# 128 bytes of unused SBUF after kt, in a kernel of band attention and two gated layers

## The chip, the cores and the metric

One core of a Trainium2 chip runs the whole program. The metric is the device time of one execution, in microseconds (us). What is read from the inside of an execution comes from one profiled execution of the kernel.

## What is computed

The reference has three parts. Only the second and third matter for the change, because TensorE (PE) spends most of its time there.

```python
# attention: 2 batches, 8 heads, 768 positions, head size 64: a band of width 16 and 24 block summaries
a = np.exp(scores_all); a = a / (np.sum(a, axis=-1, keepdims=True) + 1e-09)
x = np.matmul(a, v_all)            # then laid out as 1536 tokens x 512
# first gated layer, d_ff 1536
x = ((x @ w_a) * (x @ w_b)) @ w_out
# second gated layer, d_ff 2048
h = x @ w_in
out = (h - np.tanh(h)) @ w_out2
```

All inputs and outputs are float32.

## The kernel before

**Work and stages.** The 1536 tokens are three blocks of 512. A float32 operand of a large product is split into a high and a low part (`fp32r`), and a product of two such operands is three matmuls: high by high, high by low, low by high. One *set* in this document is the 12 matmuls that belong to one piece of 128 hidden columns: 4 slices of 128 by 3 products. Each of the 12 loads 128 x 128 stationary values (LDWEIGHTS, 512 bytes in each partition) and streams 512 moving columns (2,048 bytes in each partition).

- After a head (the first 42 us: loads, attention for the first block) the first layer runs through 3 blocks x 12 pieces. Each piece has three sets: `pos_a` and `pos_b` (both through `proj`, L370: stationary the weight tile `wsp`, moving the activations `XA` or `XB`) and `pos_o` (L398: stationary `wsp`, moving `gh` and `gl`, the high and low part of the gated product). That makes 36 sets at L398. Attention of the later blocks is planned in between.
- The second layer runs through 3 blocks x 16 pieces: `pos_h` (again `proj`, L370) and `pos_o2` (L459: stationary the gated product, moving `wsp`). `pos_h` puts the gated product's two parts into `gh` and `gl` for two pieces of every three, and into two buffers of the tag `vw` for the third (`G % 3 < 2`). That makes 48 sets at L459: 32 with `gh`, `gl` and 16 with `vw`.

```python
for kk in range(KC):
    wh, wl = (s[:, i, kk * 128 : (kk + 1) * 128] for i in range(2))
    for n, (w, xx) in enumerate(((wh, x[:, 0, kk]), (wh, x[:, 1, kk]), (wl, x[:, 0, kk]))):
        mm(dst, w, xx, start=(kk == 0 and n == 0), stop=(kk == KC - 1 and n == 2))
...
gs[1000 + G] = pair((("gh", 2), ("gl", 2)) if G % 3 < 2 else (("vw", 3), ("vw", 3)))
```

**Who makes the operands.** ScalarE (ACT) writes the high part of a weight into `wsp` (L184), VectorE (DVE) or GpSimd (POOL) the low part (L185). ACT writes `gh` (L363), DVE writes `gl` (L364) from `tg` and `gh`. The head is written out by hand (`SEQ`); the rest is ordered by a plan.

**Where the buffers lie.** One pool (`st`) lays a tag's buffers down in the order in which tags are first asked for. `kt` (K transposed, with the block maxima) takes 4 x 792 x 4 = 12,672 bytes in each partition, which is 99 x 128. The built programs place the tiles named in this document at these byte addresses in each partition:

| tag | bytes of a buffer | before | after the change | remainder by 512, before | after |
|---|---|---|---|---|---|
| qn | 2,048 | 18,720 and on | the same | 288 | 288 |
| wsp (4 buffers) | 4,096 | 28,960 and on | the same | 288 | 288 |
| XB | 16,384 | 45,344 | the same | 288 | 288 |
| kw | 2,048 | 61,728 and on | the same | 288 | 288 |
| w | 2,048 | 65,824 and on | the same | 288 | 288 |
| vw (3 buffers) | 2,048 | 139,552 and on | the same | 288 | 288 |
| XA | 16,384 | 145,696 | the same | 288 | 288 |
| kt | 12,672 | 162,080 | the same | 288 | 288 |
| x20a, x20b | 4,096 | 174,752 and on | 174,880 and on | 160 | 288 |
| stage, x21a, x21b | 4,096 | 182,944 and on | 183,072 and on | 160 | 288 |
| e | 2,048 | 203,424 and on | 203,552 and on | 160 | 288 |
| ta, tg | 2,048 | 207,776 and on | 207,904 and on | 416 | 32 |
| gh (2 buffers) | 2,048 | 215,968, 218,016 | 216,096, 218,144 | 416 | 32 |
| gl (2 buffers) | 2,048 | 220,064, 222,112 | 220,192, 222,240 | 416 | 32 |
| at (2 buffers) | 2,048 | 224,160 and on | 224,288 and on | 416 | 32 |

A slice of 128 float32 columns is 512 bytes, so every slice of a tile has its tile's remainder by 512.

Of the kernel before, what the change touches and what calls it, by code (L numbers as in the profile page):

```python
# [39 lines left out]
def band_attention_moe_kernel(ctx: ExitStack, tc: tile.TileContext, q, k, v, w_a, w_b, w_out, w_in, w_out2, out):  # L40
# [22 lines left out]
    def st(shape, tag, bufs=1, dt=F32):  # L63
        return sb.tile(shape, dt, tag=tag, bufs=bufs, name=tag)

    def pt(tag, shape=(128, 512)):
        return ps.tile(list(shape), F32, tag=tag, name=tag)
# [16 lines left out]
    def constants():  # L84
        nc.vector.memset(bsq, -math.sqrt(GA) * GB)
        nc.vector.memset(bth, -GC2)
        nc.vector.memset(qbd2, 0.0)
        nc.gpsimd.memset(qbd3, 0.0)

        for m, n, r in ((mavp, KW + 2 * NB - 8, BLK // 2), (mavg, 2 * NB - 4, BLK)):  # L90
            nc.gpsimd.memset(m, 1.0 / BLK)
            nc.gpsimd.affine_select(
                out=m, in_=m, pattern=[[-r, n]], compare_op=ALU.is_gt, fill=0.0,
                base=(n - NB) * r + 1, channel_multiplier=1,
            )
            nc.gpsimd.affine_select(
                out=m, in_=m, pattern=[[r, n]], compare_op=ALU.is_gt, fill=0.0,
                base=r - (n - NB) * r, channel_multiplier=-1,
            )
        nc.gpsimd.memset(qbd4, 0.0)  # L100
        for m, off in zip(masks, (0, WIN, 2 * WIN)):
            nc.gpsimd.memset(m[:, 0:KW], 0.0)
            nc.gpsimd.memset(m[:, KW:NK], math.log(BLK) / SC)
            for h in range(2):
                band = m[h * 64 : h * 64 + 64, 0:KW]
                nc.gpsimd.affine_select(
                    out=band, in_=band, pattern=[[1, KW]], compare_op=ALU.is_gt, fill=NEG,
                    base=WIN - off, channel_multiplier=-1,
                )
                nc.gpsimd.affine_select(  # L110
                    out=band, in_=band, pattern=[[-1, KW]], compare_op=ALU.is_gt, fill=NEG,
                    base=WIN + off, channel_multiplier=1,
                )
# [659 lines left out]
    with tc.manual_schedule():  # L773
        nc.vector.memset(qbd, 0.0)
        for _ in range(WARM):
            mm(pt("ps")[:, 0:256], qbd[:, 0, 0, :], qbd[:, 0, 0:2, :], start=True, stop=True)
        make_identity(nc, ident)
        XAv = st([128, 4, 2 * TB], "XA")
        kt[0] = st([128, NP, S + NB], "kt")
        constants()  # L780
        for n in SEQ.split():
            exec(compile(f"def op_{n}(op): op('{n}')\n", "<ops>", "exec"), globals())
            globals()["op_" + n](op)
# [50 lines left out]
```

## Time and profile before

| | |
|---|---|
| median of 3 runs | 667.28 us |
| lowest and highest run | 665.36 us, 667.33 us |
| span of the profiled execution (its own time is not listed apart from it) | 664.0 us |
| PE busy | 643.2 us (97%) |
| DVE, ACT, POOL busy | 501.9 us, 476.2 us, 209.7 us |
| PE's share of the chain that ended last | 82% |

The span goes from the first to the last instruction; a run's time is longer by what lies around it. The chain is followed back from the last instruction, at each step to what released it or to the instruction before it on its engine. Matmuls overlap, so the duration of one (some 390 ns) is longer than the time from its start to the next one's; the length of a piece of the chain is the time in which the engine moved on.

### The profile page before, as it was taken

What the parts mean: (1) busy time and instruction counts of PE and PEld (TensorE: products, weight loads), DVE (VectorE), ACT (ScalarE), POOL (GpSimd) and SP (SyncE); (2) the same over time, 40 slices, a digit from 0 to 9 for tenths busy, and PEclk for the clock granted to TensorE, in tenths of its full rate; (3) what the DMA queues carried; (4) which work ended last, traced back from release to release, by engine and by line L of the source; (5) the groups of instructions that cost most, each with busy time, mean ns of one, the idle gap of its engine ahead of it and who ended that gap; (6) DMA issues with size and microseconds to landing.
All of it is one profiled execution on the core that took longest, in us unless ns stands there. A gap on an engine that the chain in (4) does not pass through costs nothing.

```text
span 664.0 us, 9626 instructions
## 1 busy us (share of the span) xinstructions
PE 643.2 (97%) x3240; PEld 518.1 (78%) x3240; DVE 501.9 (76%) x999; ACT 476.2 (72%) x1000; POOL 209.7 (32%) x221
## 2 busy tenths in 40 slices
PE   7778999999899999999999999999999999999997
PEld 5567876888588888888888888888888888888885
DVE  5899999888675777647877748877777877777775
ACT  4899897798677687636655547777777777777774
POOL 6761231122000010101111135554444544444441
PEclk9989999999999999999999999999999999999999
DMA  9996984563414545513444200000010000000001
GB/s 203 243 237 179 250 226 128 169 216 107 102 66 124 169 152 155 144 47 112 149 140 152 68 1 0 1 0 1 1 63 1 0 1 0 32 33 1 1 0 64
DMA packets 84781, 62.11 MB, mean 94 GB/s; under 512 B 51892, under 2 KB 75444, under 8 KB 84732
## 3 DMA queue, kind: packets, MB, share of 16 engines
q1 hardware_dynamic: 84732, 61.50, 33.4%
q8 instruction: 25, 0.41, 0.3%
q14 instruction: 24, 0.20, 0.1%
HBM read 54.00 MB, written 7.34 MB: 92 GB/s over the span
## 4 chain that ended last, share of the span: by engine, by line
PE 82%; DVE 7%; ACT 4%; DMA 3%; issue 2%; SPq 1%; POOL 0%; DVEq 0%; ACTq 0%
PE acc L459 20%; PE pb L370 18%; PE pa L370 17%; PE acc L398 12%; PE pt L370 5%; PE ps L370 5%; DMA stage<-in_moe_w_in_dram 2%; PE ps L288 1%; DVE w L164 1%; PE ps L340 1%; DVE w L165 1%; PE pt L240 1%; PE pt L327 1%; DMA x20a<-in_q_dram 1%; SPq L610 1%
## 5 line engine op out<-in xcount | busy, mean ns | idle before, releaser
L185 POOL TENSOR_TENSOR wsp<-w,wsp 128x512 fp32r<-128x512 f32 x97 | 127.5, 1333 | 143.7 <-ACT wsp L184 143.7
L184 ACT ACTIVATE wsp<-w 128x512 fp32r<-128x512 f32 x201 | 121.4, 622 | 18.8 <-PE acc L398 8.6
L185 DVE TENSOR_TENSOR wsp<-w,wsp 128x512 fp32r<-128x512 f32 x104 | 75.0, 723 | 42.5 <-ACT wsp L184 42.3
L179 POOL TENSOR_SCALAR w<-w 128x512 f32<-128x512 f32 x52 | 42.0, 811 | 184.3 <-ACT w L154 184.1
L398 PE MATMUL acc<-gh,wsp 128*128 128x512 f32 x288 | 97.8, 398 | 0.5 <-ACT gh L363 0.5
L370 PE MATMUL pa<-XA,wsp 128*128 128x512 f32 x336 | 85.0, 400 | 2.8 <-ACT XA L720 2.1
L370 PE MATMUL pb<-XA,wsp 128*128 128x512 f32 x336 | 84.1, 394 | 1.4 <-DVE tg L386 1.4
L459 PE MATMUL acc<-wsp,gh 128*128 128x512 f32 x256 | 80.5, 396 | 0.0
L370 PEld LDWEIGHTS pa<-XA,wsp 128*128 128x128 f32 x336 | 63.5, 191 | 18.3 <-ACT XA L720 2.4
L370 PEld LDWEIGHTS pb<-XA,wsp 128*128 128x128 f32 x336 | 62.1, 188 | 15.0 <-ACT x21a L155 1.6
L363 ACT ACTIVATE gh<-tg 128x512 fp32r<-128x512 f32 x68 | 42.4, 623 | 33.3 <-DVE tg L386 32.9
L398 PEld LDWEIGHTS acc<-gh,wsp 128*128 128x128 f32 x288 | 53.7, 188 | 12.0 <-ACT gh L363 0.6
L370 PE MATMUL pb<-XB,wsp 128*128 128x512 f32 x240 | 61.0, 396 | 0.0
L370 PE MATMUL pa<-XB,wsp 128*128 128x512 f32 x240 | 60.4, 395 | 0.0
L398 PE MATMUL acc<-gl,wsp 128*128 128x512 f32 x144 | 57.3, 399 | 1.1 <-DVE gl L364 1.1
L459 PEld LDWEIGHTS acc<-wsp,gh 128*128 128x128 f32 x256 | 48.2, 188 | 11.1
L364 DVE TENSOR_TENSOR gl<-tg,gh 128x512 fp32r<-128x512 f32 x68 | 46.6, 686 | 9.4 <-ACT gh L363 9.3
L370 PEld LDWEIGHTS pa<-XB,wsp 128*128 128x128 f32 x240 | 44.5, 188 | 9.8 <-DVE XB L348 0.2
L370 PEld LDWEIGHTS pb<-XB,wsp 128*128 128x128 f32 x240 | 44.4, 188 | 9.5
L459 PE MATMUL acc<-wsp,gl 128*128 128x512 f32 x128 | 50.5, 394 | 0.0
L459 PE MATMUL acc<-wsp,vw 128*128 128x512 f32 x192 | 46.5, 390 | 0.0
L459 PEld LDWEIGHTS acc<-wsp,vw 128*128 128x128 f32 x192 | 35.9, 188 | 8.1 <-DVE vw L364 0.4
(304 smaller groups left out, 1176.0 us busy)
## 6 DMA issues: line engine op xcount, KB each, us to landing
stage<-in_moe_w_out_dram SPq DMA_DIRECT2D x19, 512.0 KB, 3.8
stage<-in_moe_w_in_dram SPq DMA_DIRECT2D x16, 512.0 KB, 5.6
stage<-in_moe_w_a_dram SPq DMA_DIRECT2D x8, 512.0 KB, 4.9
w<-wsc SPq DMA_DIRECT2D x16, 256.0 KB, 3.5
vw<-in_v_dram SPq DMA_DIRECT2D x19, 192.0 KB, 3.2
stage<-in_moe_w_b_dram SPq DMA_DIRECT2D x7, 512.0 KB, 5.7
wsc<-x21a SPq DMA_DIRECT2D x8, 256.0 KB, 4.9
wsc<-x21b SPq DMA_DIRECT2D x8, 256.0 KB, 5.1
```

The lines of the kernel that those rows point to most:

```text
L164: nc.vector.scalar_tensor_tensor(r, t[:, :, 1], -0x40000000, r, op0=ALU.bitwise_and, op1=ALU.bitwise_or)
L165: nc.vector.tensor_tensor(r, r, t[:, :, 0], op=ALU.add)
L179: nc.gpsimd.tensor_scalar(rf, rf, HI_HI, HI_LO, op0=ALU.min, op1=ALU.max)
L184: nc.scalar.activation(s[:, 0, :], r, AF.Copy)
L185: eng.tensor_tensor(s[:, 1, :], r, s[:, 0, :].bitcast(F32), op=ALU.subtract)
L240: mm(pp, mavg[:, NB - 4 - 4 * c : 2 * NB - 4 - 4 * c], vch.pop(c).rearrange("p h d -> p (h d)"), start=(c == 0), stop=(c == NC - 1),)
L288: mm(pp[:, p, 0:NK], qt[:, p, :], kw[:, p, :], start=True, stop=True)
L363: nc.scalar.activation(dst[0], src, AF.Copy)
L364: eng.tensor_tensor(dst[1], src, dst[0].bitcast(F32), op=ALU.subtract)
L370: mm(dst, w, xx, start=(kk == 0 and n == 0), stop=(kk == KC - 1 and n == 2))
L398: mm(acc[blk][d][:, c0:c1], w, t, start=(f == 0 and c0 == 0 and n == 0), stop=(f == F1 - 1 and n == 2))
L459: mm(a[c], g[:, cs], s[:, i, :], start=(f == 0 and n == 0), stop=(f == F2 - 1 and n == 2))
```

## The change

One more tile is asked for in the head, right after `kt`. It holds 32 float32 values in each partition, 128 bytes. Nothing reads or writes it. All tags that are first asked for later lie 128 bytes higher; those before it stay (table above).

```diff
         XAv = st([128, 4, 2 * TB], "XA")
         kt[0] = st([128, NP, S + NB], "kt")
+        st([128, 32], "pad1")
         constants()
```

On all five engines the two built programs have the same instructions in the same order with the same waits, apart from the number at the end of a buffer's name.

## Rows read from the trace of the kernel before

**Rows 1.** The page: busy time of the engines, and shares of the chain.

```profile
PE 643.2 (97%) x3240; PEld 518.1 (78%) x3240; DVE 501.9 (76%) x999; ACT 476.2 (72%) x1000; POOL 209.7 (32%) x221
...
PE 82%; DVE 7%; ACT 4%; DMA 3%; issue 2%; SPq 1%; POOL 0%; DVEq 0%; ACTq 0%
```

**Rows 2.** Windows: length, busy us and instructions by engine, clock, DMA share, GB/s.

```profile
core 0: us, PE busy (x) PEld busy (x) DVE busy (x) ACT busy (x) POOL busy (x), PEclk, DMA share, GB/s
316.00:402.00 86.00, 86.00 (x377) 70.45 (x376) 61.52 (x95) 48.75 (x86) 16.94 (x18) 1.00 0.29 97
402.00:660.00 258.00, 258.00 (x1121) 210.22 (x1120) 193.59 (x295) 192.05 (x339) 119.66 (x91) 1.00 0.03 10
```

**Rows 3.** The chain in the second layer: start us, length us, engine, tile, line.

```profile
408.68 2.80 PE acc L459 x12
411.48 2.75 PE pa L370 x12
414.23 2.72 PE acc L459 x12
416.95 2.73 PE pb L370 x12
419.67 2.80 PE acc L459 x12
422.47 2.76 PE ps L370 x12
```

**Rows 4.** Line 459 from 480 to 560 us: duration of one, ns min/median/max.

```profile
L459 PE MATMUL acc<-wsp,gh x80: 390/394/404, 485.7 to 559.8; 128*128 128x512 f32 x80
L459 PE MATMUL acc<-wsp,vw x60: 389/389/389, 480.2 to 548.9; 128*128 128x512 f32 x60
L459 PE MATMUL acc<-wsp,gl x40: 392/394/397, 486.2 to 560.0; 128*128 128x512 f32 x40
```

**Rows 5.** PE's timeline about 510 us: start us, us, instructions merged.

```profile
507.80 0.64 PE L459 MATMUL acc<-wsp,gh 128*128 128x512 f32 x2
508.27 0.39 PE L459 MATMUL acc<-wsp,gl 128*128 128x512 f32 x1
...
513.34 2.88 PE L459 MATMUL acc<-wsp,vw 128*128 128x512 f32 x12
```

**Rows 6.** The chain in the last block of the first layer.

```profile
356.36 2.79 PE acc L398 x12
359.15 2.73 PE pa L370 x12
361.89 2.72 PE pb L370 x12
364.61 2.79 PE acc L398 x12
```

**Rows 7.** The chain from 60 to 345 us, shares by line.

```profile
by line: PE pa L370 23.4%; PE pb L370 22.7%; PE acc L398 21.7%; DMA stage<-in_moe_w_in_dram 3.7%; PE ps L288 3.4%; PE ps L340 2.6%; issue 2.2%; DVE w L164 2.1%; PE pt L240 1.8%; PE pt L327 1.8%; DMA stage<-in_moe_w_b_dram 1.4%; DVE w L165 1
```

**Rows 8.** Groups by line and shape, matmuls with the gated product: count | busy us, mean ns.

```profile
L398 PE MATMUL acc<-gh,wsp 128*128 128x512 f32 x288 | 97.8, 398 | 0.5 <-ACT gh L363 0.5
...
L398 PE MATMUL acc<-gl,wsp 128*128 128x512 f32 x144 | 57.3, 399 | 1.1 <-DVE gl L364 1.1
...
L459 PE MATMUL acc<-wsp,vw 128*128 128x512 f32 x192 | 46.5, 390 | 0.0
```

**Rows 9.** Groups by line and shape on DVE and ACT, with tiles on both sides.

```profile
L364 DVE TENSOR_TENSOR gl<-tg,gh 128x512 fp32r<-128x512 f32 x68 | 46.6, 686 | 9.4 <-ACT gh L363 9.3
...
L363 ACT ACTIVATE gh<-tg 128x512 fp32r<-128x512 f32 x68 | 42.4, 623 | 33.3 <-DVE tg L386 32.9
...
L364 DVE TENSOR_TENSOR vw<-tg,vw 128x512 fp32r<-128x512 f32 x16 | 11.0, 685 | 0.7 <-ACT vw L363 0.7
...
L363 ACT ACTIVATE vw<-tg 128x512 fp32r<-128x512 f32 x16 | 9.9, 618 | 1.8 <-DVE tg L438 1.8
```

## The prediction

> **What bounds the kernel now.** First the page's shares: TensorE (PE) is busy for 643.2 of 664.0 us and holds 82% of the chain that ended last; no other engine holds over 7% [rows 1]. So a change pays, or costs, through PE or not at all. Then the windows: from 316 to 402 us and from 402 to 660 us PE is busy for the whole window at clock 1.00, which is the 2.4 GHz level, and DMA engines are busy for 29% and 3% [rows 2]. In these 344 us no wait can hide or swallow a change in PE's speed. Then the chain in order of time, which gives the time in which PE moves on by one set of 12 matmuls; the busy time can't, since matmuls overlap.
>
> What that view shows is odd. All sets have the same shape, 12 matmuls of 128 x 128 by 512, and nothing waits, yet a set at line 459 takes 2.80 us with gh and gl and 2.72 with vw (the 2.72 is the one with vw: the timeline has a vw set at 513.34, after gh sets such as the one at 507.80) [rows 3, 5]. One matmul with vw lasts 389 ns at least, at most and in the median; with gh it is 390, 394 and 404, with gl 392, 394 and 397 [rows 4]. In the first layer it is the same: 2.79 us for the set at line 398, which reads gh and gl as moving operand, against 2.72 for pb, which reads XA [rows 6]. Sets of proj (line 370) right behind a gh set take 2.75 or 2.76 us in the second layer and 2.73 in the first, though they read no gh at all: the disturbance carries over for some matmuls and then dies out [rows 3, 6].
>
> What distinguishes gh and gl from vw, XA and XB is where they lie. By the table of addresses, wsp, vw, XA and XB all leave 288 by 512, so that in each fast set the stationary and the moving operand differ by a multiple of 512 bytes. gh and gl leave 416: in each slow set the two operands differ by 128 more than a multiple of 512. Who writes them is the same (ACT the high part, DVE the low one), the op count is the same, and both roles are hit, moving at line 398 and stationary at line 459.
>
> **What the change does.** It adds no instruction, no transfer and no wait, and it moves none on any queue; the only difference is the address of everything behind kt. wsp, vw, XA, XB and w stay. gh and gl go from 128 to 256 bytes past a multiple of 512 relative to wsp. No set runs at this distance in the trace of before, so its price has to be bounded.
>
> What the present 128 costs: in the second layer 32 sets with gh and gl at 2.80 - 2.72 = 0.08 us, 2.6 us; the 32 sets of proj behind them at 0.035 on average, 1.1 us; 16 sets of proj behind vw sets at 0.01, 0.2 us. Together 3.9 us, all on the chain. In the first layer each of the 36 pieces costs 0.07 at line 398 and 0.01 at the next proj, 0.08 us. Six of them lie in the undisturbed stretch and count in full, 0.5 us. The other 30 lie before 345 us, where 21.7% of a chain of 285 us, 62 us, is at line 398 [rows 7], against 30 x 2.79 = 84 us if all of it were: 74% count, 30 x 0.08 x 0.74 = 1.8 us. The sum is 3.9 + 0.5 + 1.8 = 6.2 us. These are 432 matmuls at line 398 and 576 at line 459, of which 192 with vw [rows 8], so 816 that read gh or gl.
>
> Bounds for the new distance. From below: each of the 68 gh sets (36 and 32) takes no less than 12 x 512 columns at 2.4 GHz, 2.56 us, an estimate from the granted clock [rows 2]; that would be 6.2 + 68 x 0.16 = 17 us less than now. No set in the trace comes near it. From above: each matmul as long as the slowest one in the undisturbed stretch, 404 against 389 ns [rows 4], 0.18 us a set in place of 0.08; with the rest in proportion 6.2 x 0.18 / 0.08 = 14 us in place of 6.2, 8 us more than now. I take the value of a set with vw, 2.72, the nearest row of a well-placed pair: 0 in place of 6.2 us. The choice says that the distance matters by its remainder by 256, not by 512. For this speaks that the first 128 bytes did all the harm, and equally in both directions: the stationary slice 128 past (line 459) and 128 short (line 398) cost 0.08 and 0.07. A pattern that repeats every 256 bytes has just these two kinds of place. One that repeats every 512 would have a third, and the trace doesn't tell what it is like.
>
> The other engines: the subtraction on DVE that makes the low part takes 686 ns with tg and gh, which have the same remainder, and 685 with tg and vw, which are 128 apart; ACT's copy into gh takes 623 ns and into vw 618 [rows 9]. Their operands' distances cost nothing that can be seen, so the moved tg, ta, e, at and stage count as 0; what hides an error there is that DVE is busy for 194 and ACT for 192 of 258 us in the second layer [rows 2]. Transfers keep their sizes and order.
>
> Against the profiled execution the sum is 664.0 - 6.2 = 657.8 us of span. The median of the runs shown is 3.3 us above that span, so I forecast 667.3 - 6.2 = **661.1 us**.
>
> **The rivals.**
> 1. *Nothing changes, 667.3 us.* The slow sets are slow because of something the shift keeps: that gh and gl lie far up in the partition, above all else that large matmuls read, or a period of 512 or more in which 256 is as bad as 128. The trace can't part these from my reading, since every slow tile is both high up and 128 off. Here belongs a rule of the Trainium skill, SBUF — State Buffer, section "Who interferes with whom": PE's reads of the moving operand and of weights have independent ports and wait on no one. By it no placement matters, and the time stays 667.3. The trace speaks against the rule's reading of this case: 389 against 394 ns for the same matmul [rows 4]. That the tile is dropped or fills a gap, so that the change doesn't do what it says, is excluded by the table of addresses.
> 2. *Slower, about 671 us.* The period is 512 and its half is the worst place: weight loads and moving reads meet more often than at 128. Its place is the 68 gh sets; it decides as soon as they take over 2.80 us each. At the upper bound above it is 667.3 + 8 = 675; halfway 671. For it speaks that a penalty could grow with the distance from 0, against it that most single matmuls at 128 lie near 394, not near 404 [rows 4].
> 3. *Faster still, below 658.5 us.* The half of the period is better than 0, because the two streams then never meet; the lower end is 667.3 - 17 = 650.
>
> **How the numbers follow.** My forecast gets 0.5, rival 1 gets 0.27, rival 2 gets 0.18, rival 3 gets 0.05. A difference of 0.3%, 2.0 us, is about what a measurement of this kernel can tell from no change. Faster by more: forecast and rival 3, 0.55. Within: rival 1, 0.27. Slower: rival 2, 0.18. The forecast's own range is 659 to 663.5, from the spread of the runs shown (2 us) and from first-layer sets that may count in full or less. The 8 in 10 have to take in rival 1 and the milder half of rival 2: 658.5 to 671.
>
> **What would show it.** Right: line 459's matmuls with gh and gl at 389 ns throughout like those with vw; pieces of 2.72 in the chain at lines 459 and 398 and at the proj behind them; six sets of the second layer in 16.32 us in place of 16.56; DVE and ACT groups unchanged. Rival 1 shows the same 2.80 and 2.79 again. Rival 2 shows gh sets above 2.80 with vw sets still at 2.72. I am wrong as a whole if the time moves while line 459's matmuls with gh and vw keep their difference: then it came from DVE, ACT or the transfers.

## The result, and the profile after

The changed kernel takes 659.78 us (median of 6 runs, 659.32 to 662.95) against 666.79 us before (6 runs, 665.36 to 667.83). The ratio is 0.9913, with a 95% interval of 0.9893 to 0.9932: 0.9% faster, which is 4.5 to 7.1 us (the two medians lie 7.0 apart). The forecast was 661.1 us, which is 0.9907 of the median of 667.28 shown before.

The span fell from 664.0 to 658.2 us, by 5.8; the forecast was 6.2, to 657.8. PE's busy time took all of it, 643.2 to 637.4 us; DVE stayed at 501.9 and ACT and POOL moved by about 1 us or less [rows 1]. From the page of the changed kernel:

```profile
span 658.2 us, 9626 instructions
...
PE 637.4 (97%) x3240; PEld 518.2 (79%) x3240; DVE 501.9 (76%) x999; ACT 475.1 (72%) x1000; POOL 209.1 (32%) x221
```

The chain in the second layer of the changed kernel (start us, length us, engine, tile, line, matmuls) answers to [rows 3]:

```profile
408.93 2.72 PE pa L370 x12
411.65 2.72 PE acc L459 x12
414.37 2.72 PE pb L370 x12
417.09 2.72 PE acc L459 x12
419.81 2.72 PE ps L370 x12
422.53 2.72 PE acc L459 x12
```

Six sets take 16.32 us in place of 16.56. The chain in the last block of the first layer answers to [rows 6]:

```profile
354.53 2.72 PE acc L398 x12
357.25 2.72 PE pa L370 x12
359.97 2.72 PE pb L370 x12
362.69 2.72 PE acc L398 x12
```

Line 459 of the changed kernel from 480 to 560 us (durations in ns, min/median/max) answers to [rows 4]:

```profile
L459 PE MATMUL acc<-wsp,gh x80: 388/389/390, 482.2 to 555.2; 128*128 128x512 f32 x80
L459 PE MATMUL acc<-wsp,vw x56: 389/389/390, 493.1 to 560.0; 128*128 128x512 f32 x56
L459 PE MATMUL acc<-wsp,gl x40: 389/389/390, 482.7 to 555.4; 128*128 128x512 f32 x40
```

The matmul with gh, which had 390 to 404 ns, can no longer be told from the one with vw. Where the 5.8 us came from is read from the same view of both kernels. The first set of line 459 starts in the chain at 403.13 us before and at 400.77 after, and the last of PE's work ends at 660.08 and 654.34:

```profile
403.13 2.80 PE acc L459 x12
...
651.33 8.75 PE acc L459 x36
660.08 0.02 issue
```

```profile
400.77 2.72 PE acc L459 x12
...
645.57 5.44 PE acc L459 x24
651.01 0.03 issue
651.03 3.30 PE acc L459 x12
654.34 0.02 issue
```

(The first fence is the chain of the kernel before, the second that of the changed one.) So 2.4 us came from everything ahead of the second layer, and 256.95 - 253.57 = 3.4 us from the second layer. The last three sets of line 459, which stand side by side, gave nothing: 8.75 us before, 8.77 after.

The four groups on DVE and ACT of [rows 9] stayed within 2 ns. From the changed kernel's groups by line and shape:

```profile
L364 DVE TENSOR_TENSOR gl<-tg,gh 128x512 fp32r<-128x512 f32 x68 | 46.8, 688 | 9.1 <-ACT gh L363 8.9
L363 ACT ACTIVATE gh<-tg 128x512 fp32r<-128x512 f32 x68 | 42.4, 624 | 33.9 <-DVE tg L386 33.6
L364 DVE TENSOR_TENSOR vw<-tg,vw 128x512 fp32r<-128x512 f32 x16 | 11.0, 686 | 0.7 <-PE acc L459 0.7
L363 ACT ACTIVATE vw<-tg 128x512 fp32r<-128x512 f32 x16 | 9.9, 617 | 1.8 <-DVE tg L438 1.8
```

Another group on DVE did grow: the 48 copies by mask from `qn` into `tg` (L438) took 743 to 746 ns before and 751 to 756 after. That is 0.4 us in all, and no piece of the chain of the second layer is L438.

### The profile page after: what moved, and what is told of

Same layout as the page of the kernel before. It is cut to its first block, busy times and chain, and to the rows that moved or that the text cites. A ratio compares the mean times of both kernels' runs of the same rounds, so it can differ in the third digit from the quotient of the medians.

```text
span 658.2 us, 9626 instructions
## 1 busy us (share of the span) xinstructions
PE 637.4 (97%) x3240; PEld 518.2 (79%) x3240; DVE 501.9 (76%) x999; ACT 475.1 (72%) x1000; POOL 209.1 (32%) x221
## 4 chain that ended last, share of the span: by engine, by line
PE 83%; DVE 8%; ACT 4%; DMA 2%; issue 2%; SPq 1%; POOL 0%; DVEq 0%; ACTq 0%
PE acc L459 20%; PE pb L370 18%; PE pa L370 17%; PE acc L398 12%; PE pt L370 5%; PE ps L370 5%; PE ps L288 1%; DVE w L164 1%; PE ps L340 1%; DVE wsp L185 1%; DMA stage<-in_moe_w_in_dram 1%; DVE w L165 1%; PE pt L240 1%; PE pt L327 1%; SPq L610 1%
## 5 line engine op out<-in xcount | busy, mean ns | idle before, releaser
L459 PE MATMUL acc<-wsp,gh 128*128 128x512 f32 x256 | 78.8, 389 | 0.0
```

What stands on the lines that cost most here:

```text
L459: mm(a[c], g[:, cs], s[:, i, :], start=(f == 0 and n == 0), stop=(f == F2 - 1 and n == 2))
```

## The experiments

The time was right, but the change alone doesn't say why. Nine other tags of the table moved together with gh and gl; gh and gl changed both their own address and their distance from wsp; and one step can't tell a period of 256 from some other pattern. My theory, A: what counts is the distance between the starts of the stationary and the moving operand of a large matmul, and a multiple of 256 bytes is free. The rivals are named in each expectation. In all these kernels the instructions and their order are those of the kernel before; only unused tiles of some size are asked for in other places. A comparison is with the kernel before, timed on the same chip.

### Is it gh and gl, or what moved with them?

Two runs part them. The first moves gh, gl and at alone, from the code that first asks for gh:

```diff
             i = int(n[3])
+            if i == 2:
+                st([128, 32], "padg")
             t = st([NK, NP, 128], ("at", "gh", "gl")[i // 2], 2) if i < 6 else st([NK, NP, 128], "w", 36)
```

> The 128 unused bytes are asked for right before gh, so that of the tiles named only gh, gl and at move; tg, ta, e and stage stay at their places of before. Theory A (the distance between the stationary and the moving operand of the large matmuls, by its remainder by 256 bytes, sets PE's pace): gh and gl stand 256 from wsp's remainder again, all sets take 2.72 us, ratio to before about 0.991, 659.8 us. Theory C (the gain came from one of the other tiles that the change moves): ratio 1.00, 666.8 us, sets of lines 398 and 459 at 2.79 and 2.80 us.

Measured: 660.45 us, ratio 0.9914 (0.9892 to 0.9935), all sets at 2.72 us. The chain of this kernel in the second layer:

```profile
408.37 2.72 PE pa L370 x12
411.09 2.72 PE acc L459 x12
413.81 2.72 PE pb L370 x12
416.53 2.72 PE acc L459 x12
```

The whole gain is there with x20, stage, e, ta and tg at their old places. The second run keeps these at their new places and takes gh, gl and at 128 bytes further, by the change and the edit above together.

> The change, and 128 more unused bytes right before gh: tg, ta, e, stage and x20 stay where the change put them, gh, gl and at go on to 384 past wsp's remainder by 512. Theory A: ratio to before 1.00, 666.8 us, gh sets at 2.80 us. Theory C: ratio 0.991 as with the change, since the other tiles are at their new places.

Measured: 665.48 us, ratio 0.9995 (0.9982 to 1.0007). The gain is gone, and the chain is that of [rows 3] again:

```profile
409.63 2.80 PE acc L459 x12
412.43 2.75 PE pa L370 x12
415.18 2.72 PE acc L459 x12
417.90 2.73 PE pb L370 x12
```

Theory C falls. That at moves with gh in both runs isn't parted by them; at is read by no large matmul in the first layer (line 398), and in the second only DVE writes and reads it, while it is PE's own sets that change. The run below that makes vw slow parts them: there vw changes its remainder by 256, at keeps its own, and it is the sets with vw that become slow.

### Does any move help?

```diff
         kt[0] = st([128, NP, S + NB], "kt")
+        st([128, 64], "pad1")
```

> The unused piece after kt has 256 bytes in place of 128. Theory A: gh and gl are 384 bytes past wsp's remainder by 512, which is 128 by 256, so the slow sets are back at about 2.80 us and the ratio to before is 1.00, 666.8 us. Theory D (any move off the old addresses helps, or there is a period above 512 in which only the old place is bad): as fast as the change, ratio 0.991, 659.8 us.

Measured: 665.49 us, ratio 0.9992 (0.9977 to 1.0007), gh sets at 2.80 and 2.79 us. Theory D falls: 256 bytes bring the old time back, 128 don't.

### The address itself, or the distance?

Here the change stands, and unused bytes ahead of qn move wsp, XA, XB, vw, w and kw along with gh and gl. The same edit was run with 32 values (128 bytes), with 24 (96) and with 56 (224):

```diff
+    st([128, 32], "pad0")
     mavp = st([128, KW + 2 * NB - 8], "qn", 3)
...
         kt[0] = st([128, NP, S + NB], "kt")
+        st([128, 32], "pad1")
```

> The change, and 128 unused bytes ahead of qn as well: wsp, XA, XB, vw, w and kw go from 32 to 160 by 256, and gh and gl from 32 to 160 too, so that all distances between operands are those of the change. Theory A (the distance counts): ratio to before 0.991, 659.8 us, all sets at 2.72 us. Theory B (each operand's own address counts, and 160 by 256 is a bad place for it): all 2,448 large matmuls are at the bad place, not 816 of them, so at least 0.08 us more in each of 204 sets than with the change, 16 us more, 676 us, ratio 1.014.

Measured: 660.25 us, ratio 0.991 (0.9891 to 0.993). Line 459 (now line 460, one line further down) has 389 ns throughout:

```profile
L460 PE MATMUL acc<-wsp,gh x80: 389/389/389, 482.2 to 555.2; 128*128 128x512 f32 x80
L460 PE MATMUL acc<-wsp,vw x56: 389/389/389, 493.1 to 560.0; 128*128 128x512 f32 x56
```

gh stands here at 160 by 256, as it did in the slow kernel before. Theory B falls: 160 is no bad place when wsp is there too.

The two other sizes asked whether a better place exists for all tiles together. Even an undisturbed set takes 2.72 us, 227 ns a matmul, where the prediction's lower bound of 2.56 us a set, an estimate that no run here reaches, would be 213.

> The change, and 96 unused bytes ahead of qn: wsp, XA, XB, vw, w, kw, gh and gl all go from 32 to 128 by 256, with the distances of the change. Theory F (only distances count): ratio to before 0.991, 659.8 us, sets at 2.72 us. Theory E (a moving operand of 2,048 bytes that starts 32 bytes into a piece of 128 touches 17 such pieces, and 16 when it starts with one; a matmul takes its time by pieces, 227 ns for 17): all 204 sets at 2.72 x 16 / 17 = 2.56 us, up to 204 x 0.16 = 33 us less than with the change where PE holds the chain, 627 us, ratio 0.94.

> The change, and 224 unused bytes ahead of qn: the same tiles all start at 0 by 256, with the distances of the change. Theory F: ratio to before 0.991, sets at 2.72 us. Theory E: as with 96 bytes, 2.56 us a set and about 0.94. If only a start at 0 by 256 counts, this run is fast and the one with 96 bytes stays at 0.991.

Measured: 661.51 us, ratio 0.993 (0.9904 to 0.9957), and 660.24 us, ratio 0.9901 (0.9877 to 0.9925); all sets at 2.72 us in both. Theory E fell, and with it the hope of a version that beats the change. What makes 227 out of 213 stays open.

### Can a fast tile be made slow?

If the distance is the cause, vw, always fast so far, must become slow at gh's old distance. With the change in place, vw goes 128 bytes up, and XA by 256 so that it keeps a multiple of 256:

```diff
+    st([128, 32], "pad2")
     vwb = [st([NK, H, D], "vw", 3) for _ in range(3)]
...
+        st([128, 32], "pad3")
         XAv = st([128, 4, 2 * TB], "XA")
         kt[0] = st([128, NP, S + NB], "kt")
+        st([128, 32], "pad1")
```

> The change, and 128 unused bytes ahead of vw and 128 more ahead of XA: vw goes to 128 past wsp's remainder by 256, where gh and gl were before; gh, gl and XA stay at a multiple of 256. Theory A: the 16 sets of line 459 with vw take 2.80 us and those with gh 2.72, the reverse of before; proj behind vw 2.75; 16 x (0.08 + 0.04) = 1.9 us more than with the change, 661.7 us, ratio about 0.994. Theory G (vw is fast and gh slow because of what the tags hold or of how far up they lie): vw sets stay at 2.72, 659.8 us, ratio 0.991.

Measured: 661.85 us, ratio 0.9935 (0.9919 to 0.9951), against 661.7 expected. Line 459 is line 460 here:

```profile
L460 PE MATMUL acc<-wsp,gh x80: 389/389/389, 482.8 to 556.2; 128*128 128x512 f32 x80
L460 PE MATMUL acc<-wsp,vw x52: 390/395/404, 479.8 to 559.9; 128*128 128x512 f32 x52
L460 PE MATMUL acc<-wsp,gl x40: 389/389/389, 483.2 to 556.4; 128*128 128x512 f32 x40
```

vw has taken over gh's 390 to 404 ns, and gh vw's 389. The chain shows the set with vw at 2.80 and, behind it, proj at 2.75, which reads no vw:

```profile
411.66 2.80 PE acc L460 x12
414.46 2.75 PE pb L371 x12
417.21 2.72 PE acc L460 x12
419.93 2.72 PE ps L371 x12
422.65 2.72 PE acc L460 x12
```

So neither the height in the partition nor the tag is the cause (theory G and the first half of rival 1). The disturbance that outlasts its set was made on purpose here: XB, which the proj reads in this block, wsp and their distance are the same for the proj at 414.46 and the one at 419.93. In this kernel gh and gl stand an exact multiple of 512 from wsp, with the change alone 256 past one; their sets take 2.72 us at both.

### What do distances between 0 and 128 cost?

Five runs have an unused piece of 32, 64, 96, 160 or 192 bytes after kt; only the number in the change's one line differs.

> The unused piece after kt has 64 bytes: gh and gl go from 128 to 192 bytes past wsp's remainder, 64 short of the next multiple of 256. Theory A1 (the cost of a gh set falls with the distance to the next multiple of 256): half of the 7 us of before is left, ratio about 0.995, 663 us, gh sets at about 2.76 us. Theory A2 (every distance that is no multiple of 256 costs the same): ratio 1.00, gh sets at 2.79 and 2.80 us. Theory A3 (only the distance by 64 or 128 counts in another way): faster than 0.992 or slower than 1.005.

> The unused piece after kt has 32 bytes: gh and gl go from 128 to 160 bytes past wsp's remainder, 96 short of the next multiple of 256. Theory A1: three quarters of the 7 us are left, ratio about 0.997, gh sets at about 2.78 us. Theory A2: ratio 1.00. Theory A3: a ratio outside 0.995 to 1.005, since 32 is no multiple of 64.

> The unused piece after kt has 96 bytes. Counted as start of the stationary minus start of the moving operand by 256, line 459 is at 224 and line 398 at 32. So far: 0 gave 2.72 us a set, 64 gave 2.80, 96 gave 2.81, 128 gave 2.79 and 2.80, 160 gave 2.80, 192 gave 2.75. If the cost follows that curve, line 459 comes to 2.73 or 2.72 and line 398 to between 2.72 and 2.80; ratio 0.991 to 0.996. If only an exact multiple of 256 is free, both are at 2.75 or more; ratio 0.996 to 1.00.

> The unused piece after kt has 160 bytes: the mirror of the run with 96, line 459 at 32 and line 398 at 224. If the cost hangs on the signed distance and not on the line, line 459 takes what line 398 took with 96 bytes and line 398 what line 459 took, within 0.02 us a set. If it hangs on the line (which operand carries the moved tile), the lines keep their values of the run with 96.

> The unused piece after kt has 192 bytes, the mirror of the run with 64: line 459 at 64 and line 398 at 192 (start of the stationary minus start of the moving operand, by 256). With 64 bytes, line 459 stood at 192 and took 2.75 us, the mildest of the off places, and line 398 at 64 and took 2.80. If the signed distance sets the cost, they change places: line 398 at 2.75 and line 459 at 2.80, ratio about 0.998. If the line sets it: 2.75 at line 459 and 2.80 at line 398 again, ratio about 0.9965.

Distance is the start of the stationary minus that of the moving operand, by 256; the lengths are those of the sets in the chain, and the next column is proj right behind.

| bytes after kt | line 459: distance, set, proj | line 398: distance, set, proj | ratio (95% interval) |
|---|---|---|---|
| 0 (before) | 128, 2.80, 2.75 or 2.76 | 128, 2.79, 2.73 | 1 |
| 32 | 160, 2.80, 2.76 or 2.77 | 96, 2.81, 2.73 | 1.0017 (1.0002 to 1.0032) |
| 64 | 192, 2.75, 2.72 | 64, 2.80, 2.74 | 0.9965 (0.9952 to 0.9978) |
| 96 | 224, 2.79, 2.72 or 2.73 | 32, 2.80, 2.75 | 0.998 (0.997 to 0.999) |
| 128 (the change) | 0, 2.72, 2.72 | 0, 2.72, 2.72 | 0.9913 (0.9893 to 0.9932) |
| 160 | 32, 2.79, 2.72 or 2.73 | 224, 2.80, 2.76 | 0.9998 (0.9985 to 1.0012) |
| 192 | 64, 2.80, 2.75 | 192, 2.76, 2.77 | 1.0001 (0.999 to 1.0012) |
| 256 | 128, 2.80, 2.75 or 2.76 | 128, 2.79, 2.73 | 0.9992 (0.9977 to 1.0007) |

The rows behind the mildest place, 192, are the chain of the kernel with 64 bytes, line 459,

```profile
408.31 2.75 PE acc L459 x12
411.06 2.72 PE pa L370 x12
```

and that of the kernel with 192 bytes, line 398:

```profile
357.64 2.76 PE acc L398 x12
360.41 2.77 PE pa L370 x12
```

The smooth curve (A1) falls: 32 bytes off cost 2.79 or 2.80, as much as 128. For the set itself, that every off place costs the same (A2) nearly holds, with one exception: 192, with 2.75 and 2.76. The exception moved from line 459 to line 398 when the distances changed places, so the signed distance sets the length of the gh set and not the line. Line 398 at 192 hands its saving back in the proj behind (2.77), though; that is why the kernel with 192 bytes is no faster than before and the one with 64 is. Its ratio, 1.0001, is neither of the two that were written down (0.998 and 0.9965); neither counted the proj behind.

The sets could not part line from distance in the runs with 96 and 160 bytes, since both lines came to about 2.80 in both. The proj behind could. The chain of the kernel with 96 bytes, lines 398 (distance 32) and 459 (224):

```profile
356.53 2.80 PE acc L398 x12
359.33 2.75 PE pa L370 x12
...
408.94 2.79 PE acc L459 x12
411.73 2.72 PE pa L370 x12
```

The same of the kernel with 160 bytes, lines 398 (224) and 459 (32):

```profile
356.21 2.80 PE acc L398 x12
359.02 2.76 PE pa L370 x12
...
408.71 2.79 PE acc L459 x12
411.50 2.72 PE pa L370 x12
```

The distances changed places and the values behind the sets stayed with their lines. So the set's own length goes by the distance, but what it leaves to the next set, and with it the whole cost, hangs on the line too. Why is not shown.

Of the two guesses written down for 96 bytes, the curve missed line 459 by 0.06 (2.73 against 2.79); the other, that only an exact multiple of 256 is free, holds. Lengths in these two kernels agree within 0.01 us, and their ratios differ by 0.0018 with intervals that overlap: a difference of that size in the times alone says nothing here.

## Why the prediction was right

- **What bounds the kernel: right, but for the end.** PE's busy time and the span fell by the same 5.8 us. That no wait can swallow a change up to 660 us fails at the last set of line 459: in both kernels PE waits there for its vw, first for the part from ACT (0.3 us before, 0.4 after), then for the part from DVE (0.4 in both).
- **The choice that 256 past a multiple of 512 is as good as a multiple of 512: right.** The change, and the run with 256 bytes, bear out the period of 256 in steps of 128; the run that made vw slow shows that the distance is the cause. But the choice rested on one argument, that 128 did equal harm in both directions, and the five runs took its force: nearly every place off a multiple of 256 costs a set the same, so a period of 512 with one free place could have shown equal harm at 128 to either side as well. That 256 is free was in good part luck. What the argument did not say, and the runs showed, is that of the places tried only a multiple of 256 is free.
- **The sum: right within 0.4 us of span, by two parts of unequal worth.**
  - *Second layer: 3.9 forecast, 3.4 measured.* The measured part is firm: the two other kernels with gh 128 off a multiple of 256 take 256.96 and 256.97 us here, against 256.95, and four others with all distances at a multiple 253.54 to 253.57. "All on the chain" was too much. The two gh sets just before the last set were to gain 0.16 us; PE reaches the last set sooner and waits longer for vw. Three of the 48 sets of proj run before the first set of line 459, 0.08. The rest, 0.2, is lengths with two decimals: six sets that add up to 16.56 come to 16.545 when 24 are read at once, from 414.23 to 480.41.
  - *Ahead of it: 2.3 forecast, 2.4 measured.* That it fits so well is luck. The first set of line 459 starts at 403.13, 404.08 and 404.82 us in the three kernels with gh 128 off, so one execution of each kernel can't give this part to better than some 1.7 us, nor say whether 74% of the early sets is the right share. (Seven sets, not six, lie in the undisturbed stretch: 0.02 us.)
- **The disturbance behind a gh set: right.** The 1.1 us for proj came in with the rest (less the three sets above), and the run with vw made the same disturbance at another place.
- **Other engines at 0: right for the time.** The groups that the prediction named kept their durations within 2 ns, and the run that moved the other tiles and put gh and gl back to 128 off gained nothing. That no distance on DVE costs anything is not quite so: the copies at L438 take 742 to 748 ns in three kernels where tg and qn are 128 apart by 256 (before, gh moved alone, 256 bytes) and 747 to 757 in six where they are 0 apart. No run was made to test this, and why is open.
- **Rival 1 fell with its price, 667.3 us.** The Trainium skill's rule, SBUF — State Buffer, section "Who interferes with whom", that PE's two reads have ports of their own and wait on no one, gave this time too; the measured 659.78 us decides against using it for such matmuls. Height in the partition fell with the run in which vw became slow without leaving its neighbourhood.
- **Rivals 2 and 3 fell.** No distance tried makes a set longer than 2.81 us, so 671 us were out of reach at any of these places, and none makes it shorter than 2.72.

What is not shown is the mechanism inside PE. A weight load runs beside the matmul before it (in the kernel before, the load of gl from 508.04 to 508.23 us lies within the two matmuls with gh from 507.80 to 508.44), so the load may meet the moving reads of another matmul than its own; within a set both have the same remainder, and no run here parts them. That the two reads meet at all is an argument, not a row.

## What to carry to other kernels

Where the same matmul, with nothing waiting, is slower with one tile than with another, compare the tiles' start addresses with those of the other operand before looking at who writes them. Here a stationary and a moving operand whose starts differ by a multiple of 256 bytes gave 2.72 us a set, and every other distance tried 2.75 to 2.81. This holds for `fp32r` matmuls of 128 x 128 by 512 that follow one another without a wait; no other type or size was tried. A tile of 12,672 bytes, an odd multiple of 128, was enough to put gh and gl off; test such a thing by making a fast tile slow, since a gain alone also fits other stories.

## What was not expected

- In the set itself, 32 bytes off a multiple of 256 cost as much as 128 bytes (2.79 and 2.80 us against 2.79 and 2.80), while 192 cost half or less (2.75 and 2.76).
- The place as such counted for nothing where it was tried: with the operands moved together by 96, 128 or 224 bytes, all sets kept 2.72 us.
- A badly placed operand slows matmuls that don't read it. The proj behind a bad set took up to 2.77 us, with operands of its own that take 2.72 elsewhere.
